# Projections as column tiles, one pool of plane buffers and a two-plane addition on GpSimd in a fused attention kernel

## The chip, the cores and the metric

The kernel runs on one core of one Trainium2 chip. The metric is the device time of one execution in microseconds; the verdicts of this document compare the median of several runs. Five engines work side by side, each through its own instructions in order: TensorE (PE; its weight loads are shown as PEld), VectorE (DVE), ScalarE (ACT), GpSimd (POOL) and SyncE (SP), which issues most DMAs. They wait for each other by semaphores.

## The reference

Two independent layers on 2048 positions of width 512 with 32 heads of 16. Their outputs stand side by side.

```python
def _A_ref(x, wq, wk, wv, wo):          # one k and one v for all heads
    q = heads(x @ wq);  k = x @ wk;  v = x @ wv
    p = softmax(einsum("bhqd,bkd->bhqk", q, k) * 16 ** -0.5)
    return merge(einsum("bhqk,bkd->bhqd", p, v)) @ wo

def _B_ref(x, wqkv, w_phi, wo):         # linear attention, learned features
    q, k, v = heads(x @ wqkv)
    phi = lambda t: concat([softmax(t @ w_phi), softmax(-(t @ w_phi))])
    kv = einsum("bhsf,bhsd->bhfd", phi(k), v);  z = phi(k).sum(s)
    return merge(einsum(phi(q), kv) / (einsum(phi(q), z) + 1e-6)) @ wo

return concatenate([_A_ref(...), _B_ref(...)], axis=-1)
```

## The kernel before

**Part A, scores.** A score tile is 128 keys by 512 queries of one head, with a contraction over 32 rows (two heads of 16, one of them masked to zero in `KR`). There are 32 heads x 4 query blocks x 16 key blocks = 2048 such tiles. PE computes them in row tiles (`score`, L1701): up to four matmuls of 32 rows side by side. The queries are worked through in 32 stages `sc`, one after the other; four score tiles of a stage that share their keys are a *quad*.

The exponential of a tile is taken in one of two ways.

- **On ACT** (`expo`, L1765): one instruction turns two tiles in two PSUM banks into bf16 in `PT`. Scores go to two pairs of banks in turn, so the next pair's scores may be computed as soon as ACT has read the pair before. A quad is then summed with the values (`pv`, L1810) by four matmuls of 128 rows and 32 columns, four column tiles side by side, into the bank `ACC`.
- **On DVE and GpSimd**: DVE scales a tile and rounds it to an int16 (`bits`, L1881), whose bits read as float16 are nearly the exponential. Three more planes are made from these by adding 256, 512 and 768 to the integers (`shift`), and the four planes, each with its own constant in the weights `VK`, are summed (`d_pv`, L1957). A plane of a quad has 128 x 2048 integers. GpSimd adds as 64-bit integers (`int64_add`, L1916), DVE as int16 (L1919). How many of the three additions go to DVE follows from how far GpSimd lags (`DV`, `LATE`).

Buffers: `Z` holds the first planes of 4 quads, `Zt` 10 shifted planes.

**Projections.** All products with weight matrices (queries `pq` L1691, keys `pk` L1614, part B's `bk` L2198, `bv` L2227, `bq` L2295, `q4` L2365, `s8` L2382, output `op` L2032 and, at the end, `out_part` L2052 and L2089) are groups of up to four matmuls of 128 x 128 weights and 512 columns, issued as one block. They need one PSUM bank of the three that the DVE score tiles also use.

**What sets the order.** `plan` runs when the kernel is built. Each piece of work is a job with an engine, a booked duration, what it comes after and a priority. `run` picks the next job of each engine by when it can start (`ready`) and by its rank, which has a random part drawn from `SEEDS`, one number for each 14 us. The result is a fixed order of instructions on each engine. The planner books a switch of PE between row, column and full tiles (`mode`), and it puts empty matmuls (`fill`, L1459; `company`, L1442) where PE would be idle. `paired` and `lock` keep GpSimd's additions and DVE's plane additions, normalisations (`on`) and feature products (`ew`) apart, by a wait of GpSimd for DVE.

The share of quads that goes to DVE is not fixed either: `next_dq` opens a quad whenever DVE, banks and buffers allow it, and ACT takes the rest.

Of the kernel before, what the change touches and what calls it, by code (L numbers as in the profile page):

```python
# [1175 lines left out]
class _Fast:  # L1176
# [13 lines left out]
    NQ, NP = 4, 10  # L1190
# [3 lines left out]
    def __init__(self, nc, st, ins, out):  # L1194
# [24 lines left out]
        self.Z = sb("Z", [128, self.NQ, 4, 512], I16)  # L1219
        self.Zt = sb("Zt", [128, self.NP, 4, 512], I16)  # L1220
# [105 lines left out]

    def ready(self, j):
# [235 lines left out]
    def jobs_a(self):  # L1563
        ps, xT, job = self.ps, self.xT, self.job
        for kc in range(4):
# [17 lines left out]
        for ch in range(16):  # L1583
# [98 lines left out]
    def proj_q(self, ch):  # L1682

        ps, xT = self.ps, self.xT
        qc, A = ch // 4, ch % 4
        bank = self.bank(("pq", ch))

        def fn(pe):
            mm = None
            for dc in range(4):  # L1690
                mm = pe.matmul(ps[:, bank, :], lhsT=self.wq[:, dc, A * 128:A * 128 + 128], rhs=xT[:, dc, qc * 512:(qc + 1) * 512], start=(dc == 0), stop=(dc == 3))  # L1691
            return mm
        self.add("pe", fn, reads=self.ax(qc) + [("wq", 0 if A == 0 else 1)], writes=[("PS", bank)])
# [143 lines left out]
    def next_dq(self):  # L1837
# [3 lines left out]
        def scores():  # L1841
# [4 lines left out]
            if b is None:  # L1846
# [40 lines left out]

    def block(self, quad):
# [9 lines left out]
        self.pbusy += 3 - len(dv)
        self.zuse[quad] = 4
        self.dbusy += 0.6 * len(dv)  # L1900

        def ok():
            return bool(self.pfree) and (sc == self.dquads[self.dpvq][0] or len(self.pfree) > self.SPARE)

        def shift(eng, t):
# [769 lines left out]
```

## Time and profile before

| | |
|---|---|
| median of three runs | 681.87 us (681.83 to 682.0) |
| profiled execution | 682.29 us |
| its span, first to last instruction | 680.5 us |
| PE busy | 655.6 us |
| DVE busy | 640.5 us |
| ACT busy | 663.5 us |
| GpSimd busy | 519.8 us |
| exps on ACT | 676 of two tiles each |
| tiles on DVE | 696 |

An engine's busy time is the union of its instructions, so an instruction that waits for nothing but follows closely counts without a gap. Where an engine's instructions overlap a little, the step from start to start tells more than the mean length. For PE the ends of matmuls are modelled, so its busy share says little about how full it is.

### The profile page before, as it was taken

How to read it: one execution, taken by the hardware profiler on the slowest of the kernel's cores; microseconds unless marked ns; L12 is line 12 of the kernel's file. 1: busy time of each engine (PE TensorE's matmuls, PEld its weight loads, DVE VectorE, ACT ScalarE, POOL GpSimd, SP SyncE). 2: the span in 40 equal slices, each digit the busy share in tenths (PEclk: the TensorE clock that was granted, in tenths of full speed). 3: DMA queues.
4: the chain of work that ended last, by engine and by line, in shares of the span. 5: the costliest groups of instructions: out<-in, count | busy, mean ns of one | idle time of the engine just before them, and what ended most of it. 6: DMA issues, size and time to landing. Idle time of an engine off the chain costs nothing.

```text
span 680.5 us, 18118 instructions
## 1 busy us (share of the span) xinstructions
PE 655.6 (96%) x7538; PEld 203.0 (30%) x7595; DVE 640.5 (94%) x1071; ACT 663.5 (98%) x748; POOL 519.8 (76%) x544
## 2 busy tenths in 40 slices
PE   8999999999999999999999999999999999999997
PEld 3323333233332233322322322322223222222222
DVE  4999999999999899999899999999999999999997
ACT  5999999999999999999999999999999999999996
POOL 5688888778688858877578678688888788878781
PEclk9999999999999999999999999999999999999999
DMA  9930000000000100020030221130100001000001
GB/s 194 151 95 26 2 10 18 3 14 15 7 21 23 36 3 3 25 72 10 26 94 26 51 78 33 41 87 2 42 18 8 27 18 34 2 26 3 11 17 37
DMA packets 45543, 23.97 MB, mean 35 GB/s; under 512 B 35404, under 2 KB 41548, under 8 KB 45452
## 3 DMA queue, kind: packets, MB, share of 16 engines
q1 hardware_dynamic: 43724, 22.43, 13.7%
q8 instruction: 61, 1.00, 0.6%
q10 hardware_dynamic: 1728, 0.30, 0.2%
q14 instruction: 30, 0.25, 0.1%
HBM read 10.27 MB, written 4.96 MB: 22 GB/s over the span
## 4 chain that ended last, share of the span: by engine, by line
PE 43%; ACT 32%; DVE 19%; POOL 3%; issue 2%; DMA 1%; DVEq 0%; POOLq 0%
ACT f_PT L1765 31%; PE f_ps L1701 15%; DVE f_Z L1881 13%; PE f_ps L1957 11%; PE f_ps L1810 6%; POOL f_Zt L1916 3%; PE f_ps L2382 2%; PE f_ps L2032 1%; PE f_ps L2227 1%; DVE f_Zt L1919 1%; PE f_ps L2295 1%; ACT f_Ek L2206 1%; PE f_ps L1691 1%; PE f_ps L2198 1%; PE f_ps L2365 1%
## 5 line engine op out<-in xcount | busy, mean ns | idle before, releaser
L1765 ACT ACTIVATE f_PT<-f_ps 128x1024 bf16<-128x1024 f32 x676 | 633.4, 1082 | 4.2 <-PE f_ps L1701 2.0
L1916 POOL INT64_ADD f_Zt<-f_Z x481 | 501.0, 1042 | 127.5 <-DVE f_Z L1881 36.6
L1881 DVE TENSOR_SCALAR f_Z<-f_ps 128x512 int16<-128x512 f32 x696 | 439.0, 681 | 18.6 <-PE f_ps L1701 15.2
L1701 PE MATMUL f_ps<-f_QA,f_KR 32*128 32x512 bf16 x2048 | 283.2, 384 | 6.7 <-ACT f_PT L1765 4.0
L1957 PE MATMUL f_ps<-f_Zt,f_VK 128*32 128x512 f16 x2088 | 189.6, 385 | 2.2 <-POOL f_Zt L1916 1.4
L1701 PEld LDWEIGHTS f_ps<-f_QA,f_KR 32*128 32x128 bf16 x2048 | 74.2, 91 | 247.2 <-ACT f_PT L1765 205.8
L1810 PE MATMUL f_ps<-f_PT,f_VA 128*32 128x512 bf16 x1352 | 117.3, 385 | 0.0
L1957 PEld LDWEIGHTS f_ps<-f_Zt,f_VK 128*32 128x32 bf16 x2088 | 48.5, 94 | 78.5 <-issue 41.9
L1957 PE MATMUL f_ps<-f_Z,f_VK 128*32 128x512 f16 x696 | 67.5, 385 | 0.7 <-DVE f_accS L1465 0.5
L1810 PEld LDWEIGHTS f_ps<-f_PT,f_VA 128*32 128x32 bf16 x1352 | 27.8, 94 | 46.1 <-issue 43.8
L1919 DVE TENSOR_SCALAR f_Zt<-f_Z 128x2048 int16<-128x2048 int16 x41 | 34.1, 857 | 0.0
L1957 PEld LDWEIGHTS f_ps<-f_Z,f_VK 128*32 128x32 bf16 x696 | 17.6, 94 | 25.6 <-issue 17.4
L1465 DVE COPY f_accS<-f_ps 128x512 f32<-128x512 f32 x31 | 21.2, 682 | 0.4 <-PE f_ps L1957 0.3
L2237 DVE TENSOR_TENSOR f_vS<-f_ps,f_rs 128x1024 bf16<-128x1024 f32 x16 | 19.5, 1220 | 1.3 <-PE f_ps L2227 0.6
L2212 DVE TENSOR_REDUCE f_ssum<-f_Ek 128x64 f32<-128x1024 bf16 x16 | 19.3, 1206 | 0.1
L2302 ACT ACTIVATE f_ET<-f_ps 128x512 bf16<-128x512 f32 x32 | 18.6, 707 | 0.0
L2206 ACT ACTIVATE f_Ek<-f_ps 128x512 bf16<-128x512 f32 x32 | 17.9, 635 | 0.0
L2198 PE MATMUL f_ps<-f_Wk,f_BxT 128*128 128x512 bf16 x57 | 15.2, 381 | 1.0 <-DVE f_Z L1881 0.5
L2227 PE MATMUL f_ps<-f_Bwv,f_BxT 128*128 128x512 bf16 x55 | 14.6, 380 | 1.4 <-issue 1.0
L2382 PE MATMUL f_ps<-f_Bwo,f_ET 128*128 128x512 bf16 x55 | 14.6, 381 | 1.3 <-issue 0.8
L2295 PE MATMUL f_ps<-f_BxT,f_Wq 128*128 128x512 bf16 x53 | 13.9, 380 | 1.6 <-issue 1.0
L1459 PE MATMUL f_ps<-f_ones,f_zero 128*32 128x512 bf16 (+8 forms) x79 | 14.1, 377 | 1.3 <-POOL f_zero L1485 1.3
(105 smaller groups left out, 291.7 us busy)
## 6 DMA issues: line engine op xcount, KB each, us to landing
f_denS<-f_dd SPq DMA_DIRECT2D x15, 256.0 KB
out_dram<-f_outB SPq DMA_DIRECT2D x17, 128.0 KB, 1.9
f_Wk<-f_wd SPq DMA_DIRECT2D x4, 512.0 KB
f_Ek<-f_wd SPq DMA_DIRECT2D x4, 512.0 KB
f_accS<-f_accS SPq DMA_DIRECT2D x60, 32.0 KB
out_dram<-f_outA SPq DMA_DIRECT2D x14, 128.0 KB, 1.9
f_Bwv<-in_B_wqkv_dram SPq DMA_DIRECT2D x1, 512.0 KB
f_Bwo<-in_B_wo_dram SPq DMA_DIRECT2D x1, 512.0 KB
```

The costliest lines, as they stand in the source:

```text
L1465: self.add("dve", lambda v: v.tensor_copy(out=out, in_=in_), reads=reads, writes=writes)
L1701: return pe.matmul(self.ps[:, bank, :], lhsT=self.KR[32 * g:32 * g + 32, sc % 2, kap * 128:(kap + 1) * 128], rhs=self.QA[32 * g:32 * g + 3 ...
L1765: self.add("act", lambda a: a.activation(out=PT[:, sl[0]:sl[0] + size, :], in_=ps[:, b0:b0 + size, :], func=ACT.Exp), reads=[("PS", b0 + i ...
L1810: mm = pe.matmul(ps[32 * g:32 * g + 32, bank, :], lhsT=w, rhs=PT[:, slots[g], :], start=start, stop=stop, tile_position=(0, 32 * g))
L1881: self.add("dve", lambda v: v.tensor_scalar(out=self.Z[:, z, h, :], in0=ps[:, bank, :], scalar1=self.Z1, scalar2=self.Z0, op0=ALU.mult, op ...
L1916: self.add("pool", lambda g: g.int64_add(out=w(o), in0=w(Z), in1=256 * t * 0x0001000100010001), reads=zk, writes=[("Zp", p)], lock=True)
L1919: self.add(eng, lambda v: v.tensor_scalar(out=o, in0=Z, scalar1=256.0 * t, scalar2=None, op0=ALU.add), reads=zk, writes=[("Zp", p)], lock= ...
L1957: mm = pe.matmul(ps[32 * g:32 * g + 32, bank, :], lhsT=w, rhs=Z[:, sl[g], :], start=start, stop=stop, tile_position=(0, 32 * g))
L2198: mm = pe.matmul(ps[:, bank, :], lhsT=xT[:, dc, st * 128:(st + 1) * 128], rhs=w[:, dc, :], start=(dc == 0), stop=(dc == 3))
L2206: self.add("act", (lambda a, sg: (lambda e: e.activation(out=Ek[:, r, a].rearrange("p h f -> p (h f)"), in_=ps[:, bank, :], func=ACT.Exp, ...
L2227: mm = pe.matmul(ps[:, bank, :], lhsT=xT[:, dc, st * 128:(st + 1) * 128], rhs=w[:, dc, :], start=(dc == 0), stop=(dc == 3))
L2382: mm = pe.matmul(ps[:, bank, :], lhsT=ET[:, (8 * m + C) % 16, i * 128:i * 128 + 128], rhs=self.Bwo[:, C, :], start=(C == 0), stop=(C == 3))
```

## The change

- **Column tiles.** Every projection step, one matmul with 128 x 128 weights, becomes four matmuls with 128 x 32 weights that write partitions 0 to 31, 32 to 63 and so on of the same bank side by side, in the manner of the sums L1810 and L1957. The empty matmuls and the last output products do the same. Only the first query projection, the first block of keys and the value projection stay full.
- **Pieces.** `proj` makes two jobs of a projection of four steps: three steps, then one, so other work may stand between them. `part` emits a piece. Keys keep one piece of four, `q4` one of two.
- **One pool.** `Z` has 14 buffers for planes of any kind (`NS`); `Zt` goes. A new quad needs more than `SPARE` = 4 free ones.
- **GpSimd.** The second plane (+256) is one addition (`single`). The third and fourth come from the first and second by adding 512 to both in one instruction (`pair`), on two buffers read and two written. DVE makes planes only in the end or where GpSimd lags far.
- **Planner.** Other constants (`AHEAD`, `LATE`, `LAST`, `SPARE`, `T_B`, ranks) and other `SEEDS`; part B may run later into the span (its end mark goes from 460 to 520).

```diff
-    NQ, NP = 4, 10
+    NS = 14
-        self.Z = sb("Z", [128, self.NQ, 4, 512], I16)
-        self.Zt = sb("Zt", [128, self.NP, 4, 512], I16)
+        self.Z = sb("Z", [128, self.NS, 4, 512], I16)
...
+    CH, DL = (3, 1), 0.5
+    def proj(self, name, spec, after=(), prio=3, rel=0.0, ok=None, ch=None):
+        c0, ch = 0, ch or self.CH
+        for x, n in enumerate(ch):
+            last = x == len(ch) - 1
+            nm = name if last else ("f%d" % x,) + name
...
+            self.job(nm, "pe", self.PCO + 0.2155 * n, (lambda c0, n: (lambda: self.part(name, spec, c0, n, sum(ch), nm0)))(c0, n),
+                     after=[("f%d" % (x - 1),) + name] if x else after, mode="col", nb=0 if x else 1, prio=self.PCH if x else prio, rel=rel, ok=None if x else ok)
+            c0 += n
+    def part(self, name, spec, c0, n, N, nm0):
...
+            for c, l, r in zip(cs, ls, rs):
+                for j in range(4):
+                    mm = pe.matmul(ps[32 * j:32 * j + 32, bank, :], lhsT=l[:, 32 * j:32 * j + 32], rhs=r, start=(c == 0), stop=(c == N - 1), tile_position=(0, 32 * j))
...
-            job(("bv", st), "pe", self.PFU, self.b_projv, after=[(self.BVA, st)], mode="full", nb=1, prio=3)
+            self.proj(("bv", st), (lambda st: (lambda c: self.b_projv(st, c)))(st), after=[(self.BVA, st)])
...
-        return bool(self.zfree) and self.dve_quad() is not None and self.behind() < self.SLACK
+        return len(self.zfree) > self.SPARE and self.dve_quad() is not None and self.behind() < self.SLACK
...
-        late = max(0.0, self.te["pool"] - self.te["dve"]) + self.PDUR * (self.pbusy + 3)
-        dv = self.DV[sum(late > x for x in self.LATE)]
+        late = max(0.0, self.te["pool"] - self.te["dve"]) + self.pbusy + self.PDUR + self.PPAIR
+        mode = sum(late > x for x in self.LATE)
...
+        def pair():
+            y = self.plane[quad, 1]
...
+            o = sorted(self.slots(2))
+            for x in o:
+                self.zfree.remove(x)
+            self.plane[quad, 2], self.plane[quad, 3] = o if z < y else o[::-1]
+            v = lambda a, b: self.Z[:, a:b + 1:b - a].rearrange("p s a n -> p s (a n)").bitcast(I64)
+            self.add("pool", lambda g: g.int64_add(out=v(*o), in0=v(*sorted((z, y))), in1=512 * 0x0001000100010001), reads=keys(z) + keys(y), writes=keys(o[0]) + keys(o[1]), lock=True)
...
-    T_B = (36.0, 460.0)
+    T_B = (36.0, 520.0)
-    SEEDS = (414003, 0, 696415, 686783, 383730, 881047, 250259, 520661, 483296, 656371, 43673, 328220, 159137, 626223, 709770, 238062,
+    SEEDS = (414003, 0, 1041337, 435470, 192003, 0, 527849, 3011, 382445, 15968, 407590, 202556, 915370, 580570, 784570, 491747,
```

What the order looks like at three places, by the instructions as they stand in each program.

PE, among part B's projections. L1701 and L1726 are scores, L1957 and L2004 sums of a plane, L1810 and L1835 sums of ACT's quads, L2227 and L1354 a projection. Before:

```order
L1701 MATMUL f_ps<-f_QA,f_KR 128x512 x3
L1957 MATMUL f_ps<-f_Z,f_VK 32x512 x4
L1701 MATMUL f_ps<-f_QA,f_KR 128x512 x2
L2227 MATMUL f_ps<-f_Bwv,f_BxT 128x512 x4
L1701 MATMUL f_ps<-f_QA,f_KR 128x512 x4
```

After:

```order
L1726 MATMUL f_ps<-f_QA,f_KR 128x512 x3
L1835 MATMUL f_ps<-f_PT,f_VA 32x512 x8
L1354 MATMUL f_ps<-f_BxT,f_Wq 32x512 x12
L1835 MATMUL f_ps<-f_PT,f_VA 32x512 x4
L1726 MATMUL f_ps<-f_QA,f_KR 128x512 x4
L1835 MATMUL f_ps<-f_PT,f_VA 32x512 x4
L1354 MATMUL f_ps<-f_BxT,f_Wq 32x512 x4
L1726 MATMUL f_ps<-f_QA,f_KR 128x512 x2
```

A projection stood alone between two groups of scores; now it stands in two pieces, each beside sums of the same kind of tile.

GpSimd, between part B's small casts (L2243, L2272). ISA is `int64_add`. Before:

```order
L2243 CAST f_vS<-f_rs 128x64
L1916 ISA f_Zt<-f_Z 128x1024 x8
L2243 CAST f_vS<-f_rs 128x64
L1916 ISA f_Zt<-f_Z 128x1024 x4
L2243 CAST f_vS<-f_rs 128x64
L1916 ISA f_Zt<-f_Z 128x1024 x14
```

After (the order shows the view of two buffers as 2x1024, or as 2048 where they lie next to each other):

```order
L2272 CAST f_vS<-f_rs 128x64
L1950 ISA f_Z<-f_Z 128x1024 x2
L1968 ISA f_Z<-f_Z 128x2x1024 x2
L1950 ISA f_Z<-f_Z 128x1024
L1968 ISA f_Z<-f_Z 128x2x1024
```

Equal additions became single and wide ones in turn; there are 177 of each, for 179 quads.

DVE, shortly before the end. L1881 and L1906 are bits, L1919 plane additions, L1993 and L2037 reciprocals of row sums, L1465 and L1498 copies of `ACC`. Before:

```order
L1465 COPY f_accS<-f_ps 128x512
L1881 TENSOR_SCALAR f_Z<-f_ps 128x512 x4
L1919 TENSOR_SCALAR f_Zt<-f_Z 128x2048 x3
L1881 TENSOR_SCALAR f_Z<-f_ps 128x512 x3
L1993 RECIPROCAL f_denC<-f_denC 128x16
L1919 TENSOR_SCALAR f_Zt<-f_Z 128x2048
L1881 TENSOR_SCALAR f_Z<-f_ps 128x512 x16
```

After:

```order
L1906 TENSOR_SCALAR f_Z<-f_ps 128x512 x13
L2037 RECIPROCAL f_denC<-f_denC 128x16
L1906 TENSOR_SCALAR f_Z<-f_ps 128x512 x11
L1498 COPY f_accS<-f_ps 128x512
L1906 TENSOR_SCALAR f_Z<-f_ps 128x512 x11
L2037 RECIPROCAL f_denC<-f_denC 128x16
L1906 TENSOR_SCALAR f_Z<-f_ps 128x512 x15
```

The plane additions are gone from DVE here; six are left in its last rows.

## Rows read from the trace of the kernel before

**Rows 1.** engine totals of the page: busy us (share) xinstructions

```profile
PE 655.6 (96%) x7538; PEld 203.0 (30%) x7595; DVE 640.5 (94%) x1071; ACT 663.5 (98%) x748; POOL 519.8 (76%) x544
```

**Rows 2.** the page's chain that ended last, by engine and by line

```profile
PE 43%; ACT 32%; DVE 19%; POOL 3%; issue 2%; DMA 1%; DVEq 0%; POOLq 0%
ACT f_PT L1765 31%; PE f_ps L1701 15%; DVE f_Z L1881 13%; PE f_ps L1957 11%; PE f_ps L1810 6%; POOL f_Zt L1916 3%; PE f_ps L2382 2%; PE f_ps L2032 1%; PE f_ps L2227 1%; DVE f_Zt L1919 1%; PE f_ps L2295 1%; ACT f_Ek L2206 1%; PE f_ps L1691 1%; PE f_ps L2198 1%; PE f_ps L2365 1%
```

**Rows 3.** groups: line engine op xcount | busy us, mean ns | idle before

```profile
L1765 ACT ACTIVATE f_PT<-f_ps 128x1024 bf16<-128x1024 f32 x676 | 633.4, 1082 | 4.2 <-PE f_ps L1701 2.0
...
L1916 POOL INT64_ADD f_Zt<-f_Z x481 | 501.0, 1042 | 127.5 <-DVE f_Z L1881 36.6
...
L1881 DVE TENSOR_SCALAR f_Z<-f_ps 128x512 int16<-128x512 f32 x696 | 439.0, 681 | 18.6 <-PE f_ps L1701 15.2
...
L1957 PE MATMUL f_ps<-f_Zt,f_VK 128*32 128x512 f16 x2088 | 189.6, 385 | 2.2 <-POOL f_Zt L1916 1.4
...
L1957 PEld LDWEIGHTS f_ps<-f_Zt,f_VK 128*32 128x32 bf16 x2088 | 48.5, 94 | 78.5 <-issue 41.9
...
L1919 DVE TENSOR_SCALAR f_Zt<-f_Z 128x2048 int16<-128x2048 int16 x41 | 34.1, 857 | 0.0
```

**Rows 4.** ACT's timeline: start us, length us, instructions merged, xcount

```profile
423.57 1.08 ACT L1765 ACTIVATE f_PT<-f_ps 128x1024 bf16<-128x1024 f32 x1
424.47 3.12 ACT L2302 ACTIVATE f_ET<-f_ps 128x512 bf16<-128x512 f32 x6
...
495.21 175.96 ACT L1765 ACTIVATE f_PT<-f_ps 128x1024 bf16<-128x1024 f32 x190 [0.33 <-PE f_ps L1810]
```

**Rows 5.** the chain in order of time, from 321 us: start, us, what

```profile
321.13 0.33 PE f_ps L1810 x4
321.46 0.21 PE f_ps L1957 x4
321.68 0.33 PE f_ps L1701 x4
```

**Rows 6.** PE's timeline near 423 and 303 us, loads (PEld) and matmuls

```profile
423.13 1.90 PE L2295 MATMUL f_ps<-f_BxT,f_Wq 128*128 128x512 bf16 x8
...
302.77 0.54 PEld L1957 LDWEIGHTS f_ps<-f_Zt,f_VK 128*32 128x32 bf16 x12
302.99 0.82 PE L1957 MATMUL f_ps<-f_Zt,f_VK 128*32 128x512 f16 x12
```

**Rows 7.** windows, 569 to 656 us: all engines; then L1691 and L1881 alone

```profile
core 0: us, PE busy (x) PEld busy (x) DVE busy (x) ACT busy (x) POOL busy (x), PEclk, DMA share, GB/s
569.00:656.00 87.00, 84.74 (x946) 24.15 (x947) 84.92 (x144) 86.77 (x95) 70.98 (x69) 1.00 0.06 15
...
569.00:656.00 87.00, 0.81 (x3) 0.31 (x4) 1.00 0.06 15
...
569.00:656.00 87.00, 66.85 (x109) 1.00 0.06 15
```

**Rows 8.** who waited for whom: us in total, times, longest us

```profile
PEld f_ps L1701 <- ACT f_PT L1765: 205.8, 536, 0.8
...
PEld f_ps L1957 <- POOL f_Zt L1916: 24.9, 90, 0.7
```

**Rows 9.** GpSimd's timeline: three additions in a row

```profile
659.39 3.31 POOL L1916 INT64_ADD f_Zt<-f_Z  x3 [1.30 <-DVE f_Zt L1919]
```

**Rows 10.** groups by form: GpSimd's memsets, a full weight load

```profile
L2198 PEld LDWEIGHTS f_ps<-f_Wk,f_BxT 128*128 128x128 bf16 x64 | 5.0, 97 | 7.7 <-issue 2.6 <-DVE f_Z L1881 1.1 <-DVE f_On L2020 0.2
...
L1524 POOL MEMSET f_VK<- 128x256 bf16 x4 | 1.3, 314 | 0.2
...
L1539 POOL MEMSET f_KX<- 128x480 bf16 x1 | 0.5, 503 | 0.1
```

**Rows 11.** PE's timeline in the tail

```profile
672.44 2.12 PE L2052 MATMUL f_ps<-f_wo,f_On 128*128 128x512 bf16 x9 [0.15 <-DVE f_On L2018]
```

**Rows 12.** one tile's instructions: ns min/median/max, first and last start us

```profile
L1916 POOL INT64_ADD f_Zt<-f_Z x481: 1039/1039/1500, 23.6 to 665.8; - x161
```

More of the change, by code (lines that the diff above doesn't have):

```diff
@@ L1345, in ready @@
         if j.name[0] in ("dS", "dP"):
-            t = max(t, min([max(self.tr.get(("Zp", x), (0.0,))[0], self.tw.get(("Zp", x), (0.0,))[0]) for x in self.pfree] or [0.0]) + self.SEM)
+            n = 2 if j.name[2] == 2 and j.dur > 1.5 else 1
+            t = max(t, self.slot_at(self.slots(n)[-1]) + self.SEM)
         if j.nb:
@@ L1680, in proj_va3, with proj_q @@
                      reads=[("VK", 0, k, kc), ("VK1", 1, k)], writes=[("VK", 1, k, kc)])
-    def proj_q(self, ch):
-        ps, xT = self.ps, self.xT
+    def proj_q(self, ch, dc):
         qc, A = ch // 4, ch % 4
[L1686 to L1693, printed above, removed]
+        return self.wq[:, dc, A * 128:A * 128 + 128], self.xT[:, dc, qc * 512:(qc + 1) * 512], self.ax(qc) + [("wq", 0 if A == 0 else 1)]
     def proj_q2(self, ch):
@@ L1852, in scores @@
                 self.dleft[b] = [0, 1, 2, 3]
-                z = min(self.zfree, key=lambda x: max(self.tr.get(("Z", x, y), (0.0,))[0] for y in range(4)))
+                z = self.slots(1)[0]
                 self.zfree.remove(z)
@@ L1898, in block @@
[L1898 to L1905, printed above, removed]
+            mode = 2
+        own = (self.PDUR + self.PPAIR, self.PPAIR, 0.0)[mode]
+        self.pbusy += own
+        self.dbusy += (0.0, 0.6, 1.8)[mode]
+        self.plane[quad, 0] = z
+        for t, n in enumerate((4, 1, 1, 1) if mode == 2 else (3, 2, 1, 1)):
+            self.zuse[quad, t] = n
@@ L1906, in go, with ok, single @@
+        keys = lambda x: [("Z", x, y) for y in range(4)]
+        w = lambda x: x.rearrange("p a n -> p (a n)").bitcast(I64)
+        def ok(n, left):
+            return len(self.zfree) >= n + (left if sc == self.dquads[self.dpvq][0] else self.SPARE)
+        def single(eng, t):
             def go():
-                w = lambda x: x.rearrange("p a n -> p (a n)").bitcast(I64)
                 if self.rec is not None:
-                    self.add(eng, None, reads=zk)
+                    self.add(eng, None, reads=keys(z))
@@ new lines, in block @@
+        name = ("dS" if mode else "dP", quad, 1)
+        self.job(name, "dve" if mode else "pool", 0.60 if mode else self.PDUR, single("dve" if mode else "pool", 1), after=dz, prio=2, ok=lambda: ok(1, 2))
+        aft = {1: name}
+        if mode == 2:
+            for t in (2, 3):
+                aft[t] = ("dS", quad, t)
+                self.job(aft[t], "dve", 0.60, single("dve", t), after=dz, prio=2, ok=lambda: ok(1, 0))
+        else:
+            aft[2] = aft[3] = ("dP", quad, 2)
+            self.job(aft[2], "pool", self.PPAIR, pair, after=[name], prio=2, ok=lambda: ok(2, 0))
@@ L2084, in finish_last @@
             if k > 0:
-                self.fill(cols=(512,) * k, start=True, bank=next(b for b in self.free if b not in self.FREE0))
+                self.fill(cols=(512,) * k, start=True, mode="col", bank=next(b for b in self.free if b not in self.FREE0))
             t = max(t, ready[n])
@@ L2182, in fn @@
             for c in range(4):
-                mm = pe.matmul(ps[:, bank, c * 128:(c + 1) * 128], lhsT=wT[:, 4 * w + c, dc * 128:dc * 128 + 128], rhs=wphi[:, c, :], start=True, stop=True)
+                for j in range(4):
+                    mm = pe.matmul(ps[32 * j:32 * j + 32, bank, c * 128:(c + 1) * 128], lhsT=wT[:, 4 * w + c, dc * 128 + 32 * j:dc * 128 + 32 * j + 32], rhs=wphi[:, c, :], start=True, stop=True, tile_position=(0, 32 * j))
             return mm
```

210 lines of the change are left out of this document (93 added, 117 removed).

## The prediction, made before the changed kernel was run

> **What bounds the kernel now.** I read the engine totals first: PE, ACT and DVE are busy 94 to 98% of the span, and ACT is highest with 663.5 us [rows 1]. The chain of work that ended last goes through all three, PE 43%, ACT 32%, DVE 19%, GpSimd only 3% [rows 2]. So no engine is the bound alone. ACT sets the pace, and it falls behind its own pace where PE or DVE hands it scores late.
>
> ACT's pace is read from starts. An exp that is not held up starts 0.90 us before the next instruction (423.57 to 424.47) [rows 4]. All 676 exps take 633.4 us [rows 3], 0.937 us each, so 633.4 - 676 x 0.90 = 25 us of ACT is waiting that the busy share hides. The last 190 exps take 175.96 us; with the last one at its mean of 1.08 that is (175.96 - 1.08) / 189 = 0.925 us each [rows 4, 3]. A stretch inside them, 569 to 656 us, holds a single projection (3 recorded matmuls of L1691), and PE, DVE and ACT are all at 97% or more there [rows 7]. The other 486 exps run at (633.4 - 176) / 486 = 0.941 us.
>
> **Scores move from ACT to DVE.** All 2048 score tiles stay. In the order of the changed kernel ACT has 666 exps instead of 676, and DVE turns 716 tiles into bits instead of 696. Ten exps at 0.925 us are 9.3 us off ACT (9.0 at 0.90, 9.4 at 0.937). I take 0.925, the price in the stretch without projections.
>
> DVE pays 20 x 439.0 / 696 = 12.6 us for the new tiles, and 6 plane additions of 34.1 / 41 = 0.83 us, 5.0 us. It loses all 41 additions of L1919, 34.1 us [rows 3]. That is 16.5 us less work, and DVE can carry the new tiles. I book no further gain, since DVE's relief is what lets ACT give up the ten exps.
>
> **GpSimd.** Before, 481 additions. Three in a row take 3.31 us and one is 1.04, so one follows the next every 1.135 us [rows 9, 3]: 546 us if nothing is in between. After, 177 tile groups each get one single addition and one addition of two planes. No row shows that wide one. Its lower bound is one instruction's 1.04 us, its upper one two additions in a row, 2.27 us. GpSimd's memsets cost 0.314 us for 256 elements and 0.503 for 480 [rows 10], so time goes almost wholly with size and the fixed part is about 0.1 us. I take 2.27 - 0.1 = 2.17 as the step from one start to the next. Then GpSimd needs 177 x (1.135 + 2.17) = 585 us, between 385 and 603. That is 39 us more than before, in a shorter span; additions run from 23.6 to 665.8 us [rows 12], so 585 / 642 = 91% of their stretch against 85%. The hiding work is everything on ACT; what it costs when that cover is gone is the second rival.
>
> Pooling 4 + 10 buffers into 14 adds no instruction. It adds waits of GpSimd for PE to have read a plane. The next addition is queued behind such a wait, and PE's sums behind that. Cost zero if GpSimd keeps ahead, otherwise part of the same rival.
>
> **PE.** A projection step of 128 x 128 becomes four column tiles. I count 428 such steps of 512 columns, plus 32 short ones. Eight full matmuls take 1.90 us; with the last at about 0.39, (1.90 - 0.39) / 7 = 0.216 us a step; twelve column matmuls, three groups, take 0.82 with one at 0.39, 0.215 us a group [rows 6, 3]. The stream costs the same.
>
> The twelve column loads run in 0.54 us beside those matmuls [rows 6], so four loads (94 ns each) instead of one (97 ns) cost nothing that the stream shows [rows 3, 10]. If the four loads stood in line instead of hiding, PE would pay 428 x (4 x 0.094 - 0.097) = 120 us more. The Trainium skill, page "TensorE: Matmul & The Clock Gate", section "The mechanism", speaks for that case: a weight load overlaps matmuls in flight only when its row group differs, and column tiles share all rows. Here the trace disagrees, with twelve loads under three groups at full pace.
>
> What changes is the switch between row tiles (scores) and the rest. In the chain a sum of four column matmuls takes 0.33 us after scores but 0.21 behind another sum; scores after sums also take 0.33 [rows 5]. A change of kind therefore costs about 0.11 us. The orders hold 1335 changes of kind before and 1288 after (fills left out): 47 x 0.11 = 5.2 us saved. Split projections pay more changes where a piece stands alone, and save them where it stands beside a sum; the count has both. Against it stand 20 more groups of the DVE tiles' sums and 5 fewer of ACT's, 15 x 0.215 = 3.2 us. PE's net is 2 us less. The scores themselves are the same 2048 matmuls.
>
> Pieces also shorten the blocks. A whole projection holds PE 4 x 0.216 + 2 x 0.11 = 1.08 us, longer than an exp; three steps hold it 0.87, just under one. The price is a PSUM bank held longer. What the shorter block gives ACT is bounded from below by nothing, and from above by the pace of the stretch without projections everywhere: 486 x (0.941 - 0.925) = 8 us. I take 2 us, PE's net, because that stretch shows ACT at 0.925 even with no projections to block it, and because PE stays near full.
>
> **Clock.** The granted clock is 1.00 from 569 to 656 us, where PE did row and column tiles and almost nothing else [rows 7]. I book no loss for the full tiles that go.
>
> **The tail** keeps its steps. Nine out-projection matmuls run in 2.12 us there, beside the logarithm and exponential [rows 11]; as column tiles they keep that pace. Zero.
>
> **Sum.** The profiled execution took 682.29 us, 1.8 over its span of 680.5 and 0.4 above the median of 681.87. 682.3 - 9.3 - 2 = 671.0 for such a run, 670.6 for the median.
>
> **The rivals.**
> One, blocks were the main harm: shorter pieces bring every exp to 0.925. 682.3 - 9.3 - 8 = 665, 664.6 for the median. For it: 0.941 against 0.925 [rows 4]. Against it: PE's work barely falls, and ACT's waits may be for PE's throughput.
>
> Two, GpSimd's wide addition becomes the wait, and the kernel is slower. Planes two and three come together, so plane two is ready about 1 us later than by an addition of its own (2.17 - 1.135). PE takes its instructions in order: scores queued behind a sum that lacks its plane wait too, and ACT behind them. PE's loads of the planes' sums already waited for GpSimd 90 times, 24.9 us [rows 8], 90 of 481 additions. The same share of 177 is 33 pairs at 1.04 us, 34 us; if half reaches ACT, 670.6 + 17 = 688. It decides from 11.3 / 1.04, 11 pairs. In favour: in 569 to 656 DVE made 109 tiles, 27 groups [rows 7], which would need 27 x 3.3 = 89 us of GpSimd in 87. Against: GpSimd carries 3% of the chain [rows 2], the fourteen buffers let it run ahead, and the new order spreads its work more evenly.
>
> Three, PE is the bound and the exps only leave idle time on ACT. Then PE's 2 us are all that comes: about 680, anything from 676 to no change. For it: PE has 43% of the chain. Against it: PE's score loads wait for ACT 536 times, 205.8 us [rows 8], so PE often has time left.
>
> Four, column loads don't hide: the 120 us above, less the 25 that PE idles [rows 1], gives about 765. The 2088 column matmuls on shifted planes that already run at full pace speak against it [rows 3, 6].
>
> **How the numbers follow.** Forecast, 667 to 676: 0.50. Rival one, 660 to 667: 0.20. Rival three, 676 to 682: 0.12, half of it within 0.2% of before. Rival two: 0.15. Rival four: 0.02. Below 660: 0.01. A difference under 0.2%, 1.4 us, could not be told from none. Faster by more: 0.50 + 0.20 + 0.06 + 0.01 = 0.77; the same 0.06; slower 0.17. The range 660 to 682 leaves out rivals two and four and what is below 660, 0.18; its lower end is also every exp at about 0.918.
>
> **What would show it.** Right: 666 exps at 0.93 to 0.94 us each; bits at about 630 ns; column projections at 0.215 us a group; the wide addition near 2.1 us; L1919's work down to 6 instructions. Rival one: exps at 0.925 or less also while projections run. Rival two: PE's wait for GpSimd well above 24.9 us and GpSimd's share of the chain above 3%. Rival three: ACT's exps near 0.95 us. Rival four: projection groups above 0.3 us. A granted clock under 1.00 mid-run, or a wide addition well above 2.3 us, would make it wrong in a way not in the sum.

## The result, and the profile after it

The changed kernel takes 671.18 us (median, 670.73 to 671.34), the kernel before 681.85 us beside it (681.53 to 682.0). The ratio is 0.9843, with a 95% interval from 0.9826 to 0.986: faster by about 10.7 us. The forecast was 670.6.

The engine totals and the chain of the changed kernel (its profiled execution took 670.73 us, the span is 669.0), to be held against [rows 1, 2]:

```profile
PE 655.6 (98%) x9019; PEld 202.7 (30%) x9019; DVE 623.1 (93%) x1056; ACT 652.4 (98%) x738; POOL 538.4 (80%) x417
...
PE 53%; ACT 39%; DVE 4%; POOL 2%; DMA 1%; issue 0%; POOLq 0%
```

DVE lost 17.4 us of work, ACT 11.1; GpSimd gained 18.6. DVE's share of the chain fell from 19% to 4%. What is left is a chain of PE and ACT.

The groups (busy us, mean ns, then idle time before them and who ended it), to be held against [rows 3]:

```profile
L1790 ACT ACTIVATE f_PT<-f_ps 128x1024 bf16<-128x1024 f32 x666 | 623.0, 1100 | 3.9 <-PE f_ps L1726 2.6
L1906 DVE TENSOR_SCALAR f_Z<-f_ps 128x512 int16<-128x512 f32 x716 | 450.3, 682 | 24.5 <-PE f_ps L1726 22.0
L1968 POOL INT64_ADD f_Z<-f_Z x177 | 334.8, 1892 | 33.8 <-DVE f_ET L2373 5.4
...
L1950 POOL INT64_ADD f_Z<-f_Z x177 | 184.9, 1044 | 71.2 <-DVE f_Z L1906 35.7
L2004 PE MATMUL f_ps<-f_Z,f_VK 128*32 128x512 f16 x2864 | 234.1, 384 | 2.1 <-DVE f_accS L1498 0.8
...
L1354 PE MATMUL f_ps<-f_BxT,f_Wq 128*32 128x512 bf16 x256 | 18.9, 382 | 0.3 <-DVE f_Z L1906 0.2
```

ACT has 666 exps at 623.0 / 666 = 0.935 us (0.937 before). DVE turns 716 tiles at 450.3 / 716 = 0.629. L1968 is the addition of two planes, 1.89 us; L1950 the single one, 1.04. L2004 and L1354 are sums of planes and projections.

PE's weight loads and what they waited for (us in all, times, longest), to be held against [rows 8]:

```profile
PEld f_ps L1726 <- ACT f_PT L1790: 223.9, 568, 0.8
...
PEld f_ps L2004 <- POOL f_Z L1950: 6.6, 25, 0.5
PEld f_ps L2004 <- POOL f_Z L1968: 5.8, 20, 0.5
```

PE waits for GpSimd 12.4 us in 45 places, where it had been 24.9 in 90.

ACT's timeline near its end (start, length, operation, idle time before), to be held against [rows 4]:

```profile
539.56 119.75 ACT L1790 ACTIVATE f_PT<-f_ps 128x1024 bf16<-128x1024 f32 x129 [0.23 <-PE f_ps L1726]
```

The last 129 exps run at (119.75 - 1.10) / 128 = 0.927 us each, as the last 190 did before (0.925). But this stretch is not free of projections. The projections alone (L1354: matmuls, weight loads, then the granted clock) in its two parts:

```profile
539.50:591.00 51.50, 12.27 (x160) 3.35 (x160) 1.00 0.14 36
591.00:659.00 68.00, 0.00 (x0) 0.00 (x0) 1.00 0.07 19
```

From start to start the exps take 0.934 us in the first part, with 40 projection steps, and 0.922 in the second, with only six steps of the last output products (L2091). The 537 exps before the last 129 take (623.0 - 119.75) / 537 = 0.937 us each, where the first 486 took 0.941 before. The last exp ends at 539.56 + 119.75 = 659.31, 9.7 us before the end; it was 671.17 and 9.3.

**Where the 11.5 us of span went.** Exps 633.4 - 623.0 = 10.4. The first exp starts at 8.28 us and not at 8.83, 0.55; that step varied from 8.05 to 8.95 between kernels with the same beginning, so it belongs to the execution. The tail costs 0.4 more. About 0.9 is in ACT's other work and its gaps.

### The profile page after: what moved, and what is told of

Read it like the earlier page. It is cut to its first block, busy times and chain, and to the rows that moved or that the text cites. A ratio compares the mean times of both kernels' runs of the same rounds, so it can differ in the third digit from the quotient of the medians.

```text
span 669.0 us, 20876 instructions
## 1 busy us (share of the span) xinstructions
PE 655.6 (98%) x9019; PEld 202.7 (30%) x9019; DVE 623.1 (93%) x1056; ACT 652.4 (98%) x738; POOL 538.4 (80%) x417
## 4 chain that ended last, share of the span: by engine, by line
PE 53%; ACT 39%; DVE 4%; POOL 2%; DMA 1%; issue 0%; POOLq 0%
ACT f_PT L1790 37%; PE f_ps L1726 18%; PE f_ps L2004 16%; PE f_ps L1354 10%; PE f_ps L1835 7%; DVE f_Z L1906 2%; POOL f_Z L1968 2%; ACT f_Ek L2243 1%; DMA f_AxT<-in_A_x_dram 1%; ACT f_ET L2322 1%; PE f_ps L2333 0%; PE f_ps L1475 0%; DVE f_accS L1498 0%; DVE f_On L2064 0%; DVE f_vS L2266 0%
## 5 line engine op out<-in xcount | busy, mean ns | idle before, releaser
L1790 ACT ACTIVATE f_PT<-f_ps 128x1024 bf16<-128x1024 f32 x666 | 623.0, 1100 | 3.9 <-PE f_ps L1726 2.6
L1906 DVE TENSOR_SCALAR f_Z<-f_ps 128x512 int16<-128x512 f32 x716 | 450.3, 682 | 24.5 <-PE f_ps L1726 22.0
L1968 POOL INT64_ADD f_Z<-f_Z x177 | 334.8, 1892 | 33.8 <-DVE f_ET L2373 5.4
L1726 PE MATMUL f_ps<-f_QA,f_KR 32*128 32x512 bf16 x2048 | 277.4, 385 | 3.7 <-ACT f_PT L1790 1.6
L1950 POOL INT64_ADD f_Z<-f_Z x177 | 184.9, 1044 | 71.2 <-DVE f_Z L1906 35.7
L2004 PE MATMUL f_ps<-f_Z,f_VK 128*32 128x512 f16 x2864 | 234.1, 384 | 2.1 <-DVE f_accS L1498 0.8
L1726 PEld LDWEIGHTS f_ps<-f_QA,f_KR 32*128 32x128 bf16 x2048 | 74.1, 91 | 251.8 <-ACT f_PT L1790 223.9
L1835 PE MATMUL f_ps<-f_PT,f_VA 128*32 128x512 bf16 x1332 | 114.8, 384 | 0.0
L2004 PEld LDWEIGHTS f_ps<-f_Z,f_VK 128*32 128x32 bf16 x2864 | 57.3, 94 | 96.3 <-issue 64.9
L1835 PEld LDWEIGHTS f_ps<-f_PT,f_VA 128*32 128x32 bf16 x1332 | 28.2, 94 | 39.6 <-issue 35.1
L1498 DVE COPY f_accS<-f_ps 128x512 f32<-128x512 f32 x31 | 21.2, 684 | 1.4 <-PE f_ps L2004 0.6
L1354 PE MATMUL f_ps<-f_BxT,f_Wq 128*32 128x512 bf16 x256 | 18.9, 382 | 0.3 <-DVE f_Z L1906 0.2
L1354 PE MATMUL f_ps<-f_Bwo,f_ET 128*32 128x512 bf16 x256 | 18.9, 383 | 0.1
L1354 PE MATMUL f_ps<-f_Bwv,f_BxT 128*32 128x512 bf16 x256 | 18.9, 383 | 0.1
L2243 ACT ACTIVATE f_Ek<-f_ps 128x512 bf16<-128x512 f32 x32 | 18.7, 683 | 0.1
L1354 PE MATMUL f_ps<-f_Wk,f_BxT 128*32 128x512 bf16 x256 | 18.4, 382 | 0.0
L1354 PE MATMUL f_ps<-f_AxT,f_wq 128*32 128x512 bf16 x240 | 17.9, 383 | 0.0
L1354 PE MATMUL f_ps<-f_wo,f_On 128*32 128x512 bf16 x192 | 14.2, 383 | 0.0
L1492 PE MATMUL f_ps<-f_ones,f_zero 128*32 128x256 bf16 (+6 forms) x65 | 12.1, 357 | 1.3 <-POOL f_zero L1518 1.3
```

The lines of the kernel that those rows point to most:

```text
L1354: mm = pe.matmul(ps[32 * j:32 * j + 32, bank, :], lhsT=l[:, 32 * j:32 * j + 32], rhs=r, start=(c == 0), stop=(c == N - 1), tile_position=( ...
L1498: self.add("dve", lambda v: v.tensor_copy(out=out, in_=in_), reads=reads, writes=writes)
L1726: return pe.matmul(self.ps[:, bank, :], lhsT=self.KR[32 * g:32 * g + 32, sc % 2, kap * 128:(kap + 1) * 128], rhs=self.QA[32 * g:32 * g + 3 ...
L1790: self.add("act", lambda a: a.activation(out=PT[:, sl[0]:sl[0] + size, :], in_=ps[:, b0:b0 + size, :], func=ACT.Exp), reads=[("PS", b0 + i ...
L1835: mm = pe.matmul(ps[32 * g:32 * g + 32, bank, :], lhsT=w, rhs=PT[:, slots[g], :], start=start, stop=stop, tile_position=(0, 32 * g))
L1906: self.add("dve", lambda v: v.tensor_scalar(out=self.Z[:, z, h, :], in0=ps[:, bank, :], scalar1=self.Z1, scalar2=self.Z0, op0=ALU.mult, op ...
```

## The experiments

Two kinds: kernels that keep an order (the changed kernel's, in one case that of the kernel before) and alter one thing in it, and kernels whose order the planner makes anew. I read one number worked out from the trace for the first kind, the **late starts** of ACT: the starts that come more than 0.15 us later than 0.904 us after the exp before (0.477 after one of part B's shorter activations; both are what ACT needs when nothing holds it up). "After a projection" are those before which PE started a weight product of a projection or of part B within 1.6 us.

| kernel | us | late starts | us in them | of these after a projection |
|---|---|---|---|---|
| before | 681.85 | 43 | 10.7 | 28, 6.9 us |
| changed | 671.18 | 36 | 8.9 | 27, 6.4 us |
| full tiles again | 676.58 | 55 | 14.2 | 44, 11.3 us |
| one block of four | 676.47 | 56 | 16.2 | 49, 14.1 us |
| two additions | 701.8 | 86 | 38.7 | 42, 19.1 us |
| half sums (less work for PE) | 668.38 | 40 | 10.1 | 25, 5.8 us |

### Ten exps put back

```diff
-        return len(self.zfree) > self.SPARE and ...
+        return len(self.dquads) < 174 and len(self.zfree) > self.SPARE and ...
```

> The changed kernel with DVE limited to 174 groups of tiles as before, so ACT has 676 exps again; the order is the same until the limit is reached near the end. Theory A (the number of exps sets the time, 0.925 us each): 671.2 + 9.3 = 680 us, 679 to 682. Theory B (the gain came from elsewhere, from shorter waits): 671 to 674 us.

Measured: 679.26 us (ratio to before 0.9962, 0.9952 to 0.9971), 8.1 us more than the changed kernel. Its exps:

```profile
L1790 ACT ACTIVATE f_PT<-f_ps 128x1024 bf16<-128x1024 f32 x676 | 632.2, 1104 | 4.0 <-PE f_ps L1726 2.6
```

632.2 / 676 = 0.935 us, as with 666 exps. **Theory A holds: ACT's number of exps carries some 8 us of the gain.** The order is the changed kernel's up to about 635 us, so the ten exps come at the end. They take 632.2 - 623.0 = 9.2 us of ACT, as booked (9.3). What makes it 8.1 is the tail: from the last exp to the end it is 8.5 us here and 9.7 in the changed kernel, as ACT's next instruction there waits 0.99 us for DVE where it waited 2.24.

### Full tiles again, in the same order

```diff
-                for j in range(4):
-                    mm = pe.matmul(ps[32 * j:32 * j + 32, bank, :], lhsT=l[:, 32 * j:32 * j + 32], ..., tile_position=(0, 32 * j))
+                mm = pe.matmul(ps[:, bank, :], lhsT=l, rhs=r, start=(c == 0), stop=(c == N - 1))
```

> The changed kernel with its order of instructions kept, each projection step (both pieces) emitted as one full 128 x 128 matmul instead of four column tiles. Same 666 exps, same stream on PE; changes between kinds of tile go from 1288 to 1386. Theory A (PE is nearly full, so a change of kind is paid on the way): 98 changes at 0.10 to 0.11 us are 10 us, and most of it shows: 677 to 682 us. Theory B (PE has time left, the column form itself is worth nothing): 671 to 673 us. If column loads had cost something that the profile hides, it would be faster than 671.

Measured: 676.58 us (ratio 0.9919, 0.9902 to 0.9935), 5.4 more than the changed kernel and just under A's range. PE has 98 changes of kind more (1288 to 1386), 0.055 us for each, half of the 0.11 in the chain. Its chain and its exps:

```profile
PE 64%; ACT 31%; DVE 2%; POOL 1%; DMA 1%; issue 0%; SPq 0%; POOLq 0%
...
L1789 ACT ACTIVATE f_PT<-f_ps 128x1024 bf16<-128x1024 f32 x666 | 624.3, 1077 | 6.5 <-PE f_ps L1725 3.4
```

The late starts after a projection grow by 4.9 us, most of the 5.4: a piece beside a sum, which was one stretch of one kind, now has a change on each side.

### Column tiles alone, in the old order

```diff
+    def steps(self, pe, bank, l, r, start, stop):
+        for j in range(4):
+            mm = pe.matmul(self.ps[32 * j:32 * j + 32, bank, :], lhsT=l[:, 32 * j:32 * j + 32], rhs=r, ..., tile_position=(0, 32 * j))
...
-                mm = pe.matmul(ps[:, bank, :], lhsT=self.wq[:, dc, A * 128:A * 128 + 128], rhs=xT[...], ...)
+                mm = self.steps(pe, bank, self.wq[:, dc, A * 128:A * 128 + 128], xT[...], dc == 0, dc == 3)
```

> The kernel before with its order kept, and the projection steps of 512 columns emitted as four column tiles each. Still 676 exps. Changes of kind go from 1335 to 1309. Theory A (the column form pays only through changes of kind, at the 0.055 us each that the run with full tiles in the changed order lost): 26 x 0.055 = 1.4 us, 680.5 us, 679.5 to 682. Theory B (the column form itself helps or harms, by its loads or its power): a difference of over 3 us either way.

Measured: 681.81 us, ratio 0.9994 (0.9984 to 1.0004): no change, at the upper end of A. **Column tiles bring nothing by themselves in this order.** The old order puts its projections between scores, so only 26 changes of kind go.

### One block of four in place of three and one

```diff
+        if self.rec is None and n < N:
+            if c0:
+                ...
+                return
+            cs = range(N)
```

> The changed kernel with its order kept on every engine, but each projection in pieces of three and one now runs as one block of four steps, at the place of its first piece; nothing runs at the place of the second. PE has 50 changes of kind fewer (1288 to 1238). Theory A: pieces in themselves bring nothing, only changes of kind count: 671.2 - 50 x 0.055 = 668.4, so 667 to 671 us. Theory B, the first rival's mechanism: a block of four holds PE longer than one exp, ACT is then held up at many of the projections, and the pieces are worth it: 673 us or more, with the 666 exps at 0.938 us or more.

Measured: 676.47 us (ratio 0.9923, 0.991 to 0.9937), 5.3 more, although PE has 50 changes of kind fewer. **B holds in the time**; in one part it fails, the exps' mean stays at 0.936, since the delays show as idle time instead (6.8 us before exps, where it was 3.9):

```profile
L1797 ACT ACTIVATE f_PT<-f_ps 128x1024 bf16<-128x1024 f32 x666 | 623.2, 1075 | 6.8 <-PE f_ps L1733 5.3
```

Of ACT's starts, 21 come more than 0.3 us late (8.4 us in all), and before 18 of these stands a whole block of 16 matmuls. In the changed kernel there were 7 (3.3 us). The same place in both, PE and then ACT, first with one block:

```profile
85.23 0.39 PE L1733 MATMUL f_ps<-f_QA,f_KR 32*128 32x512 bf16 x3
85.55 0.40 PE L2011 MATMUL f_ps<-f_Z,f_VK 128*32 128x512 f16 x4
85.78 1.04 PE L1361 MATMUL f_ps<-f_Bwv,f_BxT 128*32 128x512 bf16 x16
86.75 0.71 PE L1733 MATMUL f_ps<-f_QA,f_KR 32*128 32x512 bf16 x6
...
83.95 3.06 ACT L1797 ACTIVATE f_PT<-f_ps 128x1024 bf16<-128x1024 f32 x3
87.18 1.94 ACT L1797 ACTIVATE f_PT<-f_ps 128x1024 bf16<-128x1024 f32 x2 [0.17 <-PE f_ps L1733]
```

and the changed kernel itself:

```profile
84.22 0.39 PE L1726 MATMUL f_ps<-f_QA,f_KR 32*128 32x512 bf16 x3
84.57 0.40 PE L2004 MATMUL f_ps<-f_Z,f_VK 128*32 128x512 f16 x4
84.80 0.82 PE L1354 MATMUL f_ps<-f_Bwv,f_BxT 128*32 128x512 bf16 x12
85.55 0.39 PE L1726 MATMUL f_ps<-f_QA,f_KR 32*128 32x512 bf16 x3
85.87 0.40 PE L1354 MATMUL f_ps<-f_Bwv,f_BxT 128*32 128x512 bf16 x4
86.21 0.39 PE L1726 MATMUL f_ps<-f_QA,f_KR 32*128 32x512 bf16 x3
...
83.01 4.92 ACT L1790 ACTIVATE f_PT<-f_ps 128x1024 bf16<-128x1024 f32 x5
```

From one group of scores to the next, PE needs 86.75 - 85.23 = 1.52 us with the block of four, and 1.33 and 0.66 with the pieces. ACT then idles in the one case and runs on in the other. So 0.90 us, the length of an exp, is not by itself the limit: at this place ACT, with two pairs of banks, still bore 1.33 us of absence and no longer 1.52.

### Two single additions in place of the wide one

```diff
-            self.add("pool", lambda g: g.int64_add(out=v(*o), in0=v(*sorted((z, y))), in1=512 * 0x0001000100010001), ...)
+            for src, t in ((z, 2), (y, 3)):
+                p = self.plane[quad, t]
+                self.add("pool", ... g.int64_add(out=w(self.Z[:, p]), in0=w(self.Z[:, src]), in1=512 * 0x0001000100010001) ...)
```

> The changed kernel with its order kept, the wide addition of GpSimd replaced by two single ones in a row. GpSimd gets 177 times (2.27 - 1.99) = 50 us more work; plane two is ready 0.85 us sooner, plane three 0.28 us later. Theory A (GpSimd has time left): 670 to 673 us, GpSimd's additions at about 1.04 us each. Theory B (GpSimd was close to the bound and the wide form made the rest possible): 676 us or more, with PE's waits for GpSimd well above the 12 us of the changed kernel.

Measured: 701.8 us (ratio 1.0293, 1.0276 to 1.0311), 30.6 more. **Theory A, which was mine, fell.** The totals, the chain, the additions and the waits:

```profile
PE 663.0 (95%) x9019; PEld 204.1 (29%) x9019; DVE 631.6 (90%) x1056; ACT 659.7 (94%) x738; POOL 575.2 (82%) x594
...
PE 43%; POOL 23%; DVE 20%; ACT 9%; issue 3%; DMA 1%; POOLq 0%
...
L1970 POOL INT64_ADD f_Z<-f_Z x354 | 370.2, 1046 | 47.5 <-POOL f_Z L1970 5.2
```
```profile
PEld f_ps L2006 <- POOL f_Z L1970: 36.2, 78, 1.9
...
ACT f_PT L1790 <- PE f_ps L1726: 23.6, 44, 2.2
```

GpSimd's share of the chain goes from 2% to 23% for 36.8 us more of its busy time, and its busy share, 82%, still looks free. The steps tell more. In the changed kernel a wide addition starts the next instruction 1.99 us later at the least, 2.06 in the median, and a single one 1.135, so 177 x (1.135 + 1.99) = 553 us. With two single ones it is 531 x 1.135 = 603. Fifty us more of GpSimd's steps turn into 30 us of time. (A short fall of TensorE's clock in this run, told in the last section, accounts for under 2 us of them.)

### Less work for PE

The sums of planes two to four take 256 of the 512 columns, so these planes' part is left out for half of the queries.

```diff
+                n = 256 if t and not start and not stop else 512
-                mm = pe.matmul(ps[32 * g:32 * g + 32, bank, :], lhsT=w, rhs=Z[:, sl[g], :], ...)
+                mm = pe.matmul(ps[32 * g:32 * g + 32, bank, 0:n], lhsT=w, rhs=Z[:, sl[g], 0:n], ...)
```

> The changed kernel with the sums of the second to fourth planes run over 256 of their 512 columns (the other half of the queries gets no part of these planes), order kept. PE's column stream falls from 323 to 268 us, by about 56 us; ACT, DVE and GpSimd keep their work. Theory A (PE's fullness makes ACT's exps 0.936 instead of 0.904 us): ACT's excess of about 20 us goes, 651 to 657 us. Theory B (ACT waits for other things: order, DVE, latency of one score after an exp): 666 to 671 us.

Measured: 668.38 us (ratio 0.9802, 0.9786 to 0.9818), 2.8 us less than the changed kernel, for some 56 us less of PE's stream. The totals, the chain and the exps:

```profile
PE 626.7 (94%) x9019; PEld 203.8 (31%) x9019; DVE 623.2 (94%) x1056; ACT 650.6 (98%) x738; POOL 539.6 (81%) x417
...
ACT 70%; PE 14%; DVE 8%; POOL 5%; issue 1%; DMA 1%; POOLq 0%
...
L1790 ACT ACTIVATE f_PT<-f_ps 128x1024 bf16<-128x1024 f32 x666 | 622.0, 1138 | 3.5 <-PE f_ps L1726 2.8
```

PE's share of the chain falls from 53% to 14%, and the time hardly moves. ACT's late starts are no fewer either: 40 with 10.1 us, against 36 with 8.9. **PE's throughput is not the bound**; its share of the chain showed that PE is the link, not that it is short. Theory B holds. A short fall of TensorE's clock in this run, told in the last section, does not hide a larger gain: the four executions had mean clocks from 0.995 to 0.999 and took 668.2 to 668.8 us, the one at 0.995 being the shortest. What still delays exps is, at the places read, the fixed order: PE waits in it for another engine's data, and scores stand behind. One such place, a weight load of PE behind DVE, the scores' load, and then ACT:

```profile
411.22 0.55 PEld L1354 LDWEIGHTS f_ps<-f_Bwo,f_ET 128*32 128x32 bf16 x16 [0.81 <-DVE f_Z L1906]
412.19 0.10 PEld L1726 LDWEIGHTS f_ps<-f_QA,f_KR 32*128 32x128 bf16 x3 [0.42 <-ACT f_PT L1790]
...
412.63 1.94 ACT L1790 ACTIVATE f_PT<-f_ps 128x1024 bf16<-128x1024 f32 x2 [0.53 <-PE f_ps L1726]
```

The projection waits 0.81 us for DVE to empty its bank, the scores come after it, and ACT idles 0.53.

### Orders made anew, without the drawn numbers

Six kernels have an empty `SEEDS`, so that ranks have no random part. `T_B` is part B's end mark.

```diff
-    SEEDS = (414003, 0, 1041337, ...)
+    SEEDS = ()
```

The kernel before:

> The kernel before with the searched numbers taken away (no SEEDS), so the planner's order without its random part: 686 exps. Theory A (the count of exps sets the time): 681.9 + 10 x 0.925 = 691 us, 689 to 694. Theory B (the search shortened waits and did not only move tiles): 695 us or more.

The changed kernel, mark at 520, and the same with whole blocks (`CH` of four):

> The changed kernel with the searched numbers taken away: 674 exps, 12 less than the kernel before without them. Theory A (the count of exps sets the time): 671.2 + 8 x 0.925 = 678.6 us, 676 to 681, 12 us under the kernel before without its numbers. Theory B (the new order's gain is the search's): no more than 3 us under the kernel before without numbers, 688 us or more.

> The changed kernel without searched numbers and with projections in one piece of four steps, still as column tiles, planned anew: 676 exps, 2 more than with pieces. Theory A (blocks do no harm beyond the count): 678.6 + 2 x 0.925 = 680.5 us, 678 to 683, an exp at about 0.936 us. Theory B (whole blocks hold scores up): exps at 0.945 us or more, 686 us or more.

The changed kernel with the mark at 460; the same with whole blocks; the first with single additions, planned as such:

> The changed kernel with no drawn numbers in the ranks, and part B's end mark back at 460; the planner's order has 676 exps. Theory A: the 24.6 us tail of the same kernel with the mark at 520 came from the mark. Then first exp at 8.3, 676 exps at 0.935 = 632 us, 29 to 36 us of ACT's other work and waits, a tail of about 10 and 1.8 around the span: 681 to 688 us. Theory B: without the drawn numbers part B is late whatever the mark: 695 us or more, with 15 us or more from the last exp to the end.

> As the one before it, but each projection as one block of four steps in place of three and one; the planner's order has 674 exps. Theory A: pieces of projections matter little in themselves, so the time goes with the exps, 2 x 0.9 us under that of the kernel with pieces: between 4 us below it and 2 us above. Theory B: a block of four holds PE longer than one exp and each of ACT's waits for it shows: 5 us or more above, with exps at 0.945 us or more.

> As the first of these three, but the third and fourth plane by two single additions, and the planner knows it and makes its order for them (680 exps, 4 more). Theory A: the wide addition is needed only by an order planned for it; an order planned for single additions pays for the four exps it adds, 3 to 7 us more than the first. Theory B: GpSimd with 1.135 us for each of about 520 additions is short whatever the order: 15 us or more above the first, with GpSimd and DVE together over 20% of the chain.

| kernel without drawn numbers | us | ratio (95%) | exps | us each | last exp to end |
|---|---|---|---|---|---|
| before | 693.8 | 1.0173 (1.0156 to 1.019) | 686 | 0.936 | 9.8 |
| changed, mark 520 | 701.21 | 1.0281 (1.0264 to 1.0298) | 674 | 0.935 | 24.6 |
| whole blocks, 520 | 699.54 | 1.0257 (1.024 to 1.0274) | 676 | 0.934 | 17.6 |
| changed, mark 460 | 696.48 | 1.0217 (1.02 to 1.0234) | 676 | 0.933 | 13.1 |
| whole blocks, 460 | 713.19 | 1.0458 (1.044 to 1.0475) | 674 | 0.935 | 34.0 |
| single additions, 460 | 717.07 | 1.0508 (1.0491 to 1.0526) | 680 | 0.936 | 15.2 |

The exps run at the same pace in all of them. What differs is the number of exps, the tail, and a few long gaps. The kernel before came out as theory A said; with ten more exps it takes 11.7 us more than the same kernel with its drawn numbers. The changed kernel with the mark at 520 did not, with either kind of block: both times lie where theory B put them (688 us or more, 686 or more). The exps keep the pace of theory A, but part B ends after them. The last rows with the mark at 520 (L1354 is part B's output projection), and with whole blocks and 460:

```profile
673.58 1.03 ACT L1790 ACTIVATE f_PT<-f_ps 128x1024 bf16<-128x1024 f32 x1
...
683.60 3.64 PE L1354 MATMUL f_ps<-f_Bwo,f_ET 128*32 128x512 bf16 x64
...
691.44 0.42 ACT L2104 ACTIVATE f_ET<-f_ET 128x256 f32<-128x256 f32 x1 [16.83 <-DVE f_ET L2102]
```
```profile
675.67 2.96 ACT L1790 ACTIVATE f_PT<-f_ps 128x1024 bf16<-128x1024 f32 x3
...
680.45 13.12 PE L1492 MATMUL f_ps<-f_ones,f_zero 128*32 128x512 bf16 x240
...
681.49 1.23 DVE L2373 TENSOR_TENSOR f_ET<-f_ET,f_Ek 128x2048 bf16<-128x2048 bf16 x1 [0.87 <-DMA f_Ek<-f_wd]
694.05 2.48 DVE L1498 CAST f_ET<-f_ps 128x512 bf16<-128x512 f32 x4 [11.33 <-PE f_ps L1354]
...
704.50 0.42 ACT L2104 ACTIVATE f_ET<-f_ET 128x256 f32<-128x256 f32 x1 [25.87 <-DVE f_ET L2102]
```

In the second, the order puts 240 empty matmuls (L1492), 13.1 us of PE, ahead of part B's next product, although DVE's last feature product for it (L2373) ended at 682.7 us; DVE then idles 11.33 us. So some 10 us of that tail come from the planner's filling.

The mark at 460 brings the tail from 24.6 to 13.1 us, so the mark is part of the cause. The time, 696.48 us, is all the same in theory B's range (695 or more), though without B's tail of 15 us or more: ten starts of ACT are over 0.3 us late, 15.7 us in all. Whole blocks with the mark at 460 are 16.7 us worse, yet not by B's mechanism, since the exps keep their pace; the tail alone is some 21 us longer, the empty matmuls with it. With whole blocks at 520 it is the other way by 1.7 us. So these pairs say nothing clear on blocks. Single additions lose 20.6 us also when planned for, with DVE and GpSimd at 24% of the chain (theory B): 25 starts of ACT are over 0.3 us late, 30.5 us in all.

**What follows:** without its drawn numbers the changed planner makes orders (696.48 to 717.07 us) that are slower than that of the planner before, made in the same way (693.8). The changed kernel's 10.7 us need an order picked for its parts. Taking a part out of that order costs time, but no run gives the kernel before newly drawn numbers of its own. So how much of the 10.7 us the parts bring, and how much a better draw alone would have brought, is not shown.

## Why the prediction was right

The time, 671.18 against 670.6, lies in the likeliest case. The steps did less well than the sum: that it came within 0.6 us is partly luck, since the ten exps gave 8.1 us for the 9.3 booked and all the rest 2.6 for 2.

- **Scores moved from ACT to DVE: right.** Putting ten exps back adds 9.2 us to ACT (9.3 booked) and 8.1 to the time, as the tail gets shorter. DVE fell by 17.4 us (16.5 booked), and its tiles took 0.629 us.
- **PE's 2 us: about the right size from the wrong reason.** I counted changes of kind and passed the saving on to ACT. One block of four has 50 changes fewer and is 5.3 us slower; full tiles have 98 more and are 5.4 slower; column tiles in the old order have 26 fewer and change nothing. What fits all three, though no run varies it alone, is how long PE stays away from scores at one place. From the pace of the exps before the last stretch, 0.937 us against 0.941, some 537 x 0.004 = 2 us came back, but the trace does not say by which part of the change. PE's total work is not what ACT gets back: 56 us less of it gave 2.8.
- **Rival one: its mechanism is real, its size is not.** "I take 2 us ... because that stretch shows ACT at 0.925 even with no projections to block it" undervalues the pieces, which are worth 5.3 us in this order. The exps still run at 0.935, and at 0.934 where projections stand in the last stretch, so its sign (0.925 or less also there) did not come and it gave no 665. The 0.925 itself came from 190 exps among which seven projections stand (28 loads of L1691 and L2032 from 502 to 576 us), not from the stretch with one, which runs at 0.923. The kernel before had whole blocks and only 5 starts more than 0.3 us late (2.2 us), and its late starts after a projection, 6.9 us, are hardly more than the 6.4 after the change: an order made for blocks of four can place them. So the 5.3 us are what pieces are worth here, not what they would add to the order before.
- **The wide addition: mis-sized.** 2.17 us a step was booked; it is 1.99 and the instruction takes 1.89, less than two single ones by 2 x 1.135 - 1.99 = 0.28 us. GpSimd's demand was 553 us, not 585.
- **GpSimd's cover: the step that failed most, unseen in the result.** "Against: GpSimd carries 3% of the chain" was a weak ground for giving rival two 0.15. The upper bound that I named for the wide addition, 2.27, is what the experiment with two additions has, and it costs 30.6 us: rival two, at 701.8 rather than 688. It missed because the instruction was faster than booked. At the booked 585 us GpSimd would have been 18 us from that case, and the forecast with it in doubt.
- **Rival three (PE is the bound): refuted** by exps at 0.935 and by the experiment with less work for PE.
- **Rival four (column loads stand in line): refuted.** Projections start as the sums do, three groups of a piece in 0.82 us, the same as twelve matmuls of a sum before [rows 6]. The Trainium skill, page "TensorE: Matmul & The Clock Gate", section "The mechanism", lists a weight load as overlapping matmuls in flight only when its row group differs. The trace disagrees: 256 projection matmuls whose loads share all rows keep PE busy for 18.9 us, less than their loads alone would take in line (256 x 0.095 = 24 us).
- **Clock and tail: right** within 0.4 us. From 8 us to the last exp the granted clock was 1.00, the level of 2.4 GHz, in each long stretch.
- **"The new order spreads its work more evenly": not shown as such.** PE's wait for GpSimd halved, but with the same parts, orders without the drawn numbers cost 25 to 30 us. Which of the draws' choices bring that stays open. Nor was each part, or the kernel before, tried with an order newly searched for it; an edit to a picked order can lose time just because the order was picked for something else.

## What to carry to other kernels

Where engines share one fixed order, ask how long an engine stays away from the work that the pacing engine needs, against that engine's period and the buffers between them; here its total work and the number of switches said little. An engine's share of the chain is no measure of its reserve: take the step from start to start times the count against the span, and price both ends of an unknown step. A kernel whose order was picked by search must be judged with its order, since the same parts in an unpicked order can be slower than the kernel before. And read an order made anew for empty work before blaming a part: here 13 us of one loss were fillers.

## What the runs showed of the hardware

- GpSimd's 64-bit addition over two planes (128 x 2 x 2048 int16 values) takes 1.89 us, 0.19 less than two of 1.04, and starts the next 0.28 sooner than two would.
- Four weight loads of 32 columns hide under their matmuls as one load of 128 does: a piece of three full steps and one of twelve column matmuls both take 0.82 us, and the twelve loads of the second take 0.42 us beside them.
- TensorE's granted clock fell from 1.00 (2.4 GHz) to 0.50 (1.2 GHz) for a moment in two of the experiments that kept the changed kernel's order. With half sums it was 0.50 from 342.6 to 345.8 us; before it, PE did scores, half sums and empty matmuls, busy 11.25 of the 12 us from 330 to 342. Eight matmuls of a sum took 0.96 us across the fall, where eight take 0.61 at 1.00. With two additions it was 0.50 from 72.1 to 75.3 us, soon after PE had idled 2.38 us for GpSimd. Why it fell in the first case is not shown.

Rows for the second and the third point: full tiles again, the changed kernel, half sums, two additions.

```profile
302.85 0.82 PE L1353 MATMUL f_ps<-f_BxT,f_Wq 128*128 128x512 bf16 x3
...
84.70 0.42 PEld L1354 LDWEIGHTS f_ps<-f_Bwv,f_BxT 128*32 128x32 bf16 x12
...
342.60:345.80 3.20, 3.20 (x30) 0.72 (x22) 2.96 (x6) 3.12 (x4) 2.85 (x3) 0.50 0.04 8
...
70.80 0.62 PE L2006 MATMUL f_ps<-f_Z,f_VK 128*32 128x512 f16 x8 [2.38 <-POOL f_Z L1950]
72.10:75.30 3.20, 3.20 (x26) 0.51 (x19) 0.99 (x2) 2.59 (x4) 2.93 (x3) 0.50 0.00 0
```
